# Scores from the seventh pair on as full 128-row matmuls, and V in four blocks

## The chip, the cores and the metric

The kernel runs on one core of a Trainium2 chip. The metric is the device time of one execution in microseconds (us). The core has a matrix engine (TensorE: PE for its matmuls, PEld for its weight loads), a vector engine (VectorE, DVE), a scalar engine (ScalarE, ACT), a general one (GpSimd, POOL) and a queue that issues all transfers of this kernel (SyncE, SP). The operands lie in SBUF (128 partitions); matmuls write to PSUM.

## The reference

Eight batches of twelve heads of attention with 448 positions and head size 64, with normalised queries and keys, and behind it a two-layer network without bias whose activation is h cos h:

```python
q_n, k_n = rmsnorm(q, g_q), rmsnorm(k, g_k)          # x / sqrt(mean(x*x) + 1e-6) * g
scores = q_n @ k_n.T / sqrt(64)
attn = exp(scores - max); attn = attn / (sum(attn) + 1e-9)
x = (attn @ v) with heads side by side               # 3584 x 768
h = x @ w_in                                         # 768 x 2048
out = (h * cos(h)) @ w_out                           # 2048 x 768
```

All is float32. The two weight matrices come as 64-bit numbers that the kernel turns into float32 itself.

## The kernel before

**Pairs.** Two heads make a pair `u`, 48 in all, six to a batch (NP = 6). Head 0 lies on partitions 0 to 63 of the transposed queries and keys, head 1 on 64 to 127. The 2 x 448 rows of queries are cut into seven tiles of 128: tiles 0 to 2 are head 0, tiles 4 to 6 head 1, and tile 3 is the last 64 rows of both, with the other head's part zero, so that it contracts over 128 partitions while the other six contract over 64.

**High and low parts.** The first six pairs are "plain": their matmuls take float32 operands. From the seventh pair on each operand is split into a high part (rounded to float32r) and a low part (the rest), and a product is three matmuls: high x high, low x high, high x low. `score` (L410) issues them for a pair of tiles (j, j + 4) in turn, so six matmuls with 64 contraction rows, or three for tile 3. I call the six a group; a pair has three groups.

**A pair's steps.** `st_load` to `st_pow` (L293 to L309) square and sum queries and keys and make 1/rms (`r`); `st_store` and `rk_load` send the keys' part through HBM and back as rows (`rkb`); `k_norm`, `k_high`, `k_low` and `q_scale`, `q_high`, `q_low` (L356 to L382) make the operands. After `score`, DVE scales each tile and takes its minimum (`rowmin`, L428), ACT takes the exponential and its row sums (`expo`, L435) into a tile `P`. `transp` (L459) turns the P tiles on PE in four column blocks kc of 128 (the last two overlap), seven transposes each; in block 1 one more transposes the row sums (L464), and DVE then adds 1e-9 and takes the reciprocal of the 7 x 128 result (`rs_copy`, L443). `pt_high` and `pt_low` split the turned block on ACT and DVE, and `av` (L481) multiplies it with V, which lies in five blocks per head (NVC): seven matmuls for a head, spread 2, 2, 1, 2 over the blocks.

**The network.** `ffn1` (L547) multiplies the previous batch's x with w_in in chunks fc of 128 columns, 18 matmuls a chunk, between the attention's steps; `weights` decodes w_in on DVE in four steps of a chunk (L210, L212, L214, L218), `weights2` makes seven sums of quarters of w_out. After the last pair a second plan runs the last batch's first layer and then the second layer (L613), as seven products for two batches.

**What sets the order.** `Plan` is a list scheduler that runs when the program is built. Each step is added with an engine, an assumed cost, a due time, what it reads and writes, and for transfers an assumed time to land; `order()` writes the steps down one after the other as they would start by these numbers, and this fixes the order of every engine and of SP's transfers. `RING` says how many buffers a name has. At run time each engine takes its instructions in that order and waits on semaphores. PSUM tile `PT` (two banks, L454) serves all transposes, and also the squares of the first two pairs' keys (`kn_square`).

Of the kernel before, what the change touches and what calls it, by code (L numbers as in the profile page):

```python
# [23 lines left out]
class Plan:  # L24
# [6 lines left out]
    SIGNAL = 0.16  # L31
# [33 lines left out]
    def order(self):  # L65
# [21 lines left out]
        while True:  # L87
# [35 lines left out]
def tile_attention_moe(  # L123
# [17 lines left out]
    NVC = 5  # L141
# [41 lines left out]
    def g_fold():  # L183
# [99 lines left out]
    pair = {}  # L283

# [29 lines left out]
    def kn_load(u):  # L314
        nc.sync.dma_start(tl(u, "kn", [128, 512], F32, "ql")[:KB], kn_in[u])
# [23 lines left out]
    def kn_copy(u):  # L339
        nc.scalar.activation(tl(u, "khi", [128, S], F32), kn_bank(u)[:, :S], AF.Copy, scale=gsc)  # L340
# [15 lines left out]
    def k_norm(u):  # L356
        kd = pair[u]["kd"]
        kn = tl(u, "khi", [128, S], F32) if u < NP else kd
        nc.gpsimd.tensor_tensor(kn, kd, pair[u].pop("rkb"), ALU.mult)
# [7 lines left out]

    def q_load(u):
        q = tl(u, "qhi" if u < NKT else "qd", [128, 512], F32)
        nc.sync.dma_start(q, qT[u])  # L370

    def q_scale(u):
        qd = pair[u]["qd"]
        q = tl(u, "qhi", [128, 512], F32) if u < NP else qd
        nc.gpsimd.tensor_scalar(q, qd, gsc, 0.0, op0=ALU.mult, op1=ALU.add)
# [34 lines left out]
    def score(u, j):  # L410
        d = pair[u]
        ops = (("qhi", "khi"), ("ql", "khi"), ("qhi", "kl"))[: 1 if u < NP else 3]
        if j == 0:
            tl(u, "sm", [128, 3, NQT], F32)
# [5 lines left out]
        for n, (a, c) in enumerate(ops):  # L420
            for t in tiles:
                p0, p1 = (0, 128) if t == 3 else (0, 64) if t < 3 else (64, 128)
                nc.tensor.matmul(  # L423
                    d["S", t][:, :S], d[a][p0:p1, j * 128 : j * 128 + 128], d[c][p0:p1, :],
                    start=(n == 0), stop=(n == len(ops) - 1),
                )
# [15 lines left out]

    def rs_copy(u):  # L443
        rt = tl(u, "rt", [NQT, 128], F32)
        nc.vector.tensor_scalar(rt, pt[:NQT, 896:1024], 1e-9, None, op0=ALU.add)
        nc.vector.reciprocal(rt, rt)
# [12 lines left out]
    def transp(u, kc, tiles, last):  # L459
        for t in tiles:  # L460
            src = pair[u][f"P{t}"][:, KS[kc] : KS[kc] + 128]
            nc.tensor.transpose(pt[:, t * 128 : t * 128 + 128], src, ident)  # L462
        if last:
            nc.tensor.transpose(pt[:NQT, 896:1024], pair[u]["sm"][:, 2, :], ident)  # L464

    def pt_high(u, kc, hh):
        d = pair[u]
        hi = d["hi", kc, hh] = apool.tile([128, S], F32R, tag="hi", name=f"hi{u}_{kc}_{hh}", bufs=RING["hi"])
        nc.scalar.copy(hi, pt[:, hh * S : hh * S + S])  # L469

    def pt_low(u, kc, hh):
# [6 lines left out]
        else:  # L478
            nc.vector.tensor_tensor(d["hi", 2, hh][:64], src[:64], hi.bitcast(F32)[:64], ALU.subtract)  # L479

    def av(u, kc, hh):  # L481
# [4 lines left out]
        ops = (((0, "hi", 0), (0, "lo", 0)), ((1, "hi", 1), (1, "lo", 1)), ((3, "lo", 2),), ((2, "hi", 3), (4, "hi", 2)))  # L486
        for n, (c, what, kb) in enumerate(ops[kc]):
            st = d["vs"][:, hh * NVC + c].rearrange("p a d -> p (a d)")
            nc.tensor.matmul(O, st, d.pop((what, kb, hh)), start=(kc + n == 0), stop=(kc + n == 4))  # L489

    def pt_copy(u, kc, hh):
        p = pair[u]["hi", kc, hh] = apool.tile([128, S], F32, tag="hi", name=f"hi{u}_{kc}_{hh}", bufs=RING["hi"])
        if hh:
            nc.vector.tensor_copy(p, pt[:, hh * S : hh * S + S])
        else:
            nc.scalar.copy(p, pt[:, hh * S : hh * S + S])

    def av_plain(u, kc, hh):
# [3 lines left out]
        p, st = d.pop(("hi", kc, hh)), d["vs"][:, hh * NVC + (0, 1, 3, 2)[kc]]  # L502
# [4 lines left out]
    xs = {}  # L507
# [153 lines left out]
    def weights(fc):  # L661
        d = ffn_due(0, 3 * fc) - 6.0
        w, f = ("w", fc), ("wf", fc)
        begin = 8.0 + 6.0 * fc
        add(SP, ISS, d - 30.0, w_load, fc, w=[w if f64 else f], land=8.0, start=begin)
        if f64:
            for step, eng, cost in ((0, DVE, 0.6), (1, DVE, 1.05), (2, DVE, 1.0), (3, ACT, 0.92), (4, DVE, 1.1)):
# [9 lines left out]
    def weights2(c):  # L677
# [4 lines left out]
        for k in range(4):  # L682
            st, f, e = ("wf", NFC + 4 * c + k), qk[k], d + 0.1 * span * k
            if f64:
                add(SP, ISS, e - 20.0, v_fetch, c, k, w=[st], land=LAND, start=e - 30.0)
                for step, eng, cost in ((0, DVE, 0.42), (1, DVE, 0.7), (2, DVE, 0.7), (3, ACT, 0.56), (4, DVE, 0.66)):
# [10 lines left out]
        for n, (name, src, _) in enumerate(SPLITS):  # L697
# [8 lines left out]
            add(ACT, 0.5, e, v_split, c, p, src, False, r=[f], w=[o])  # L706
# [3 lines left out]
    def prepare(u):  # L710
# [3 lines left out]
        if turned:  # L714
            kn, rn, kb = [("ql", u)], [("rn", u)], [("pt", 0, n) for n in ((0,) if u == 0 else (1, 2))]
# [6 lines left out]
            add(ACT, 0.53, D0 - 50, kn_copy, u, r=kb + [("gsc", 0)], w=khi)  # L722
# [3 lines left out]
        add(SP, ISS, D0 - 44 if turned else D0 - 30, q_load, u, w=qhi if turned else qd, land=3.5 if turned else LAND)  # L726
        add(ACT, 0.6 if turned else 0.95, D0 - 40, st_square, u, w=sd)
        add(DVE, 0.7 if turned else 1.08, D0 - 38, st_reduce, u, r=sd, w=r)
        add(POOL, 1.5 if turned else 2.6, D0 - 34, st_pow, u, w=r)
# [290 lines left out]
```

## Time and profile before

| | |
|---|---|
| median of 3 runs | 1469.57 us (1469.06 to 1471.99) |
| the profiled execution | 1471.15 us, of it the span from first to last instruction 1469.4 us |
| mean granted TensorE clock | 0.995 |
| PE, DVE, ACT, POOL busy | 96%, 75%, 62%, 46% of the span |
| transfers | 260.96 MB, mean 178 GB/s |

A row of the timeline gives start and duration of merged instructions (xN is their number), engine, line, operation, out<-in. Matmuls overlap their neighbours, so the time that one takes from the engine is the distance between starts, not its duration. A row of the groups ends with the busy time, the mean of one in ns, and the idle time before them. A row of the windows gives busy time and number of instructions of PE, PEld, DVE, ACT and POOL in that stretch, then the granted clock, the busy share of the transfer engines and GB/s.

### The profile page before, as it was taken

The page shows a single profiled execution, that of the slowest core. Times are in us where ns is not written, and L with a number is a line of the kernel's source. Part 1 is how long each engine was busy: PE and PEld are TensorE (multiplying, and loading weights), DVE is VectorE, ACT ScalarE, POOL GpSimd, SP SyncE. Part 2 cuts the span into 40 slices and gives each one's busy share as a digit, 9 for nine tenths or more (in the row PEclk, how much of TensorE's full clock was granted, in tenths as well). Part 3 has the DMA queues.
Part 4 walks back from the last instruction along what each step waited for, and adds up shares of the span by engine and source line. Part 5 has one row for each costly group of instructions (what it writes and reads, how often), then busy time and mean ns, then how long its engine had stood idle before and what let it go on. Part 6 is the DMA issues. An engine that isn't in the chain of part 4 may idle for free.

```text
span 1469.4 us, 22204 instructions
## 1 busy us (share of the span) xinstructions
PE 1407.9 (96%) x7370; PEld 1161.3 (79%) x7370; DVE 1103.2 (75%) x1861; ACT 915.1 (62%) x1820; POOL 669.0 (46%) x634
## 2 busy tenths in 40 slices
PE   5878999999999999999999999999999999999998
PEld 2334788878788878878887888878999999999998
DVE  6988898687868787777878666543958978979843
ACT  4666676767677776677776766545737547447421
POOL 4889874866776776686586765211000000000000
PEclk9999999999999999999999999999999999999999
DMA  6773344556445554646454533118948658568534
GB/s 228 223 221 117 121 129 131 184 165 210 154 153 176 179 183 148 196 145 195 157 192 157 177 111 98 59 45 310 300 159 278 229 162 303 197 193 308 162 106 142
DMA packets 135876, 260.96 MB, mean 178 GB/s; under 512 B 21792, under 2 KB 89968, under 8 KB 135760
## 3 DMA queue, kind: packets, MB, share of 16 engines
q1 hardware_dynamic: 135760, 259.53, 54.6%
q8 instruction: 58, 0.95, 0.3%
q14 instruction: 58, 0.48, 0.1%
HBM read 196.74 MB, written 62.73 MB: 177 GB/s over the span
## 4 chain that ended last, share of the span: by engine, by line
PE 81%; DVE 9%; POOL 3%; issue 3%; ACT 2%; DMA 2%; SPq 0%; POOLq 0%; ACTq 0%; DVEq 0%
PE y L625 9%; PE y L624 9%; PE y L623 9%; PE O L489 9%; PE ph L556 8%; PE PT L462 8%; PE ph L557 8%; PE ph L558 8%; PE S L423 7%; DVE S L430 2%; DVE lo L477 1%; PE y L557 1%; PE y L558 1%; PE y L556 1%; POOL r L309 1%
## 5 line engine op out<-in xcount | busy, mean ns | idle before, releaser
L438 ACT ACTIVATE P<-S,sm 128x448 f32<-128x448 f32 x336 | 213.7, 639 | 122.1 <-DVE S L430 118.4
L556 PE MATMUL ph<-xs,wi 128*128 128x448 f32 x672 | 263.6, 392 | 2.7 <-ACT he L568 2.7
L557 PE MATMUL ph<-xs,wi 128*128 128x448 f32 x672 | 247.1, 368 | 0.4 <-POOL xs L542 0.4
L558 PE MATMUL ph<-xs,wi 128*128 128x448 f32 x672 | 246.5, 367 | 0.0
L624 PE MATMUL y<-g,wo 128*128 128x448 f32 x672 | 245.6, 365 | 0.0
L625 PE MATMUL y<-g,wo 128*128 128x448 f32 x672 | 245.5, 365 | 0.0
L623 PE MATMUL y<-g,wo 128*128 128x448 f32 x672 | 245.5, 365 | 0.0
L430 DVE TENSOR_SCALAR_CACHE_REDUCE S<-S,r 128x448 f32<-128x448 f32 x336 | 220.4, 683 | 19.4 <-PE S L423 15.9
L469 ACT CAST hi<-PT 128x448 fp32r<-128x448 f32 x336 | 165.4, 535 | 91.1 <-PE PT L462 45.1
L603 ACT CAST g<-gq 128x896 fp32r<-128x896 f32 x112 | 105.7, 943 | 174.4 <-PE y L625 161.2
L477 DVE TENSOR_TENSOR lo<-PT,hi 128x448 fp32r<-128x448 f32 x252 | 143.1, 607 | 70.5 <-ACT hi L469 66.1
L601 DVE TENSOR_TENSOR g<-gq,g 128x896 fp32r<-128x896 f32 x112 | 122.1, 1090 | 83.8 <-ACT g L603 83.3
L462 PEld LDWEIGHTS PT<-ident,P 128*128 128x128 f32 x1344 | 157.7, 142 | 31.7 <-issue 20.0
L462 PE MATMUL PT<-ident,P 128*128 128x128 f32 x1344 | 182.5, 276 | 0.2 <-ACT P L438 0.2
L556 PEld LDWEIGHTS ph<-xs,wi 128*128 128x128 f32 x672 | 127.1, 189 | 27.7 <-issue 11.3
L558 PEld LDWEIGHTS ph<-xs,wi 128*128 128x128 f32 x672 | 126.7, 189 | 11.1
L623 PEld LDWEIGHTS y<-g,wo 128*128 128x128 f32 x672 | 126.3, 188 | 10.0
L625 PEld LDWEIGHTS y<-g,wo 128*128 128x128 f32 x672 | 126.3, 188 | 9.9
L624 PEld LDWEIGHTS y<-g,wo 128*128 128x128 f32 x672 | 126.3, 188 | 9.9
L557 PEld LDWEIGHTS ph<-xs,wi 128*128 128x128 f32 x672 | 127.3, 189 | 8.5 <-POOL xs L542 0.8
L309 POOL TENSOR_TENSOR r<-r,nhalf 128x14 f32<-128x14 f32 (+1 forms) x48 | 125.9, 2622 | 4.0
L489 PE MATMUL O<-hi,vs 128*128 128x448 f32 x336 | 113.2, 389 | 6.4 <-DVE hi L479 3.4
(94 smaller groups left out, 2569.4 us busy)
## 6 DMA issues: line engine op xcount, KB each, us to landing
wo<-wo_d SPq DMA_DIRECT2D x152, 384.0 KB
h_d<-he SPq DMA_DIRECT2D x128, 224.0 KB
gq<-h_d SPq DMA_DIRECT2D x64, 448.0 KB
wo_d<-ao SPq DMA_DIRECT2D x56, 384.0 KB
sd<-sd SPq DMA_DIRECT2D x46, 448.0 KB
vd<-v SPq DMA_DIRECT2D x84, 160.0 KB
raw<-w_in SPq DMA_DIRECT2D x16, 768.0 KB
rawo<-w_out SPq DMA_DIRECT2D x32, 384.0 KB
```

Source lines behind the costliest of these rows:

```text
L430: nc.vector.tensor_scalar(d["S", t][:, :S], d["S", t][:, :S], d["r"][:, t : t + 1], None, op0=ALU.mult, op1=ALU.min, accum_out=d["sm"][:, ...
L438: nc.scalar.activation(tl(u, f"P{t}", [128, S], F32, "P"), d.pop(("S", t))[:, :S], AF.Exp, bias=sm[:, 1, t : t + 1], scale=-1.0, accum_out ...
L462: nc.tensor.transpose(pt[:, t * 128 : t * 128 + 128], src, ident)
L469: nc.scalar.copy(hi, pt[:, hh * S : hh * S + S])
L477: nc.vector.tensor_tensor(lo, src, hi.bitcast(F32), ALU.subtract)
L489: nc.tensor.matmul(O, st, d.pop((what, kb, hh)), start=(kc + n == 0), stop=(kc + n == 4))
L556: nc.tensor.matmul(ph[:, :S], whi, x2[:, 0, :], start=(cc == 0), stop=False)
L557: nc.tensor.matmul(ph[:, :S], whi, x2[:, 1, :], start=False, stop=False)
L558: nc.tensor.matmul(ph[:, :S], wlo, x2[:, 0, :], start=False, stop=(cc == NCC - 1))
L623: nc.tensor.matmul(y, whi, hi[:, e], start=first and e == 0, stop=False, **more)
L624: nc.tensor.matmul(y, whi, lo[:, e], start=False, stop=False, **more)
L625: nc.tensor.matmul(y, wlo, hi[:, e], start=False, stop=last and e == NG - 1, **more)
```

## The change

From pair 6 on, the 64 contraction rows of a head are doubled to 128: `m_place` puts the keys' high part on partitions 0 to 63 and its low part on 64 to 127 of a tile `M`, `d_place` puts the queries' high part on both halves of a tile `D`, `e_place` puts the queries' low part on the upper half (0 to 63) of a tile `E` whose other half was set to zero at the start. One matmul D x M then gives high x high + high x low, and one E x M gives low x high: two matmuls with 128 rows for each of the six tiles, and still three for tile 3. The places are filled by transfers from SBUF to SBUF, ten of 64 partitions for a pair. `score` is now issued tile by tile; the plain pairs keep the old form (`score_plain`).

V lies in four blocks. The last transposed block (kc = 3) has 64 columns only, its high part on partitions 0 to 63 and its low part on 64 to 127 of one tile, against V rows that are stored twice; `av` is 2, 2, 2, 1 matmuls for a head.

The reciprocal of the row sums is taken before they are turned, on 128 x 7 numbers (`rsum`: an ACT step adds 1e-9, a DVE step takes the reciprocal); `rs_copy` only copies. The six plain pairs' queries have their own tile `q6` and are loaded at the start. The second pair's keys `kn` are loaded into another buffer than before. Loads of w_in start at other times, ring sizes and the plan's assumed costs change.

```diff
-    NVC = 5
+    NVC = 4
...
-        "sd": 1, "r": 5, "rkb": 1, "kd": 1, "kl": 2, "khi": 2, "qd": 1, "ql": 2, "qhi": 2, "vd": 1, "vs": 2, "S": 3, "sm": 3, "P": 12,
-        "hi": 4, "lo": 2, "O": 1, "xf": 6, "rs": 1, "rt": 1, "ph": 1, "he": 2, "wf": 2, "rn": 1,
-        "aq": 4, "at": 2, "ao": 2,
+        "sd": 1, "r": 5, "rkb": 1, "kd": 1, "kl": 1, "khi": 1, "qd": 1, "ql": 1, "qhi": 1, "M": 3, "D": 3, "E": 3, "vd": 1, "vs": 2, "S": 3, "sm": 3, "P": 11,
+        "hi": 4, "lo": 2, "O": 1, "xf": 6, "rs": 1, "rt": 1, "ph": 1, "xsb": 1, "he": 2, "wf": 2, "rn": 1,
+        "aq": 4, "at": 2, "ao": 1,
...
+    def m_place(u, h, low):
+        if not low:
+            pair[u]["M", h] = apool.tile([128, S], F32R, tag="M", name=f"M{u}_{h}", bufs=RING["M"])
+        src = pair[u]["kl" if low else "khi"].bitcast(F32)
+        nc.sync.dma_start(pair[u]["M", h].bitcast(F32)[64 * low : 64 * low + 64], src[64 * h : 64 * h + 64])
+
+    def d_place(u, h):
+        t = pair[u]["D", h] = apool.tile([128, 384], F32R, tag="D", name=f"D{u}_{h}", bufs=RING["D"])
+        src = pair[u]["qhi"].bitcast(F32)[64 * h : 64 * h + 64, :384]
+        for a in (0, 64):
+            nc.sync.dma_start(t.bitcast(F32)[a : a + 64], src)
...
+    ORDER = (3, 0, 4, 1, 5, 2, 6)
+
+    def score(u, n):
...
+            h, c = t // 4, t % 4 * 128
+            ops = tuple((d[name, h][:, c : c + 128], d["M", h]) for name in ("D", "E"))
+        for i, (a, c) in enumerate(ops):
+            nc.tensor.matmul(d["S", t][:, :S], a, c, start=(i == 0), stop=(i == len(ops) - 1))
...
-        rt = tl(u, "rt", [NQT, 128], F32)
-        nc.vector.tensor_scalar(rt, pt[:NQT, 896:1024], 1e-9, None, op0=ALU.add)
-        nc.vector.reciprocal(rt, rt)
+        nc.vector.tensor_copy(tl(u, "rt", [NQT, 128], F32), pt[:NQT, 896:1024])
...
     def transp(u, kc, tiles, last):
+        n = 128 if kc < 3 else 64
         for t in tiles:
-            src = pair[u][f"P{t}"][:, KS[kc] : KS[kc] + 128]
-            nc.tensor.transpose(pt[:, t * 128 : t * 128 + 128], src, ident)
+            src = pair[u][f"P{t}"][:, KS[kc] : KS[kc] + n]
+            nc.tensor.transpose(pt[:n, t * 128 : t * 128 + 128], src, ident)
...
-        begin = 8.0 + 6.0 * fc
+        begin = 4.0 + 3.0 * fc if fc < 3 else 24.0 + 7.0 * fc
...
-            kn, rn, kb = [("ql", u)], [("rn", u)], [("pt", 0, n) for n in ((0,) if u == 0 else (1, 2))]
+            kn, rn, kb = [("qd" if u == 0 else "ql", u)], [("rn", u)], [("pt", 0, n) for n in ((0,) if u == 0 else (1, 2))]
```

Three places of the order are spoken of below. The first is PE in the middle of the attention, where the score matmuls of a pair stand between chunks of the first layer (`ph`), products with V (`O`) and transposes (`PT`). Before, a group of two tiles:

```order
L558 MATMUL ph_11_5329<-xs,wi_1486 128x448
L423 MATMUL S_1_5386<-khi_5069,qhi_5106 128x448
L423 MATMUL S_5_5387<-khi_5069,qhi_5106 128x448
L423 MATMUL S_1_5386<-khi_5069,ql_5141 128x448
L423 MATMUL S_5_5387<-khi_5069,ql_5141 128x448
L423 MATMUL S_1_5386<-kl_5075,qhi_5106 128x448
L423 MATMUL S_5_5387<-kl_5075,qhi_5106 128x448
L489 MATMUL O_5400<-hi_0_0_5378,vs_5097 128x448
```

Now, tile 5 (head 1) and tile 2 (head 0) of a pair:

```order
L603 MATMUL ph_4_6321<-xs,wi_735 128x448
L465 MATMUL S_5_6426<-M_1_6205,D_1_6210 128x448
L465 MATMUL S_5_6426<-M_1_6205,E_100 128x448
L465 MATMUL S_2_6433<-M_0_6054,D_0_6065 128x448
L465 MATMUL S_2_6433<-M_0_6054,E_99 128x448
L534 MATMUL O_6306<-hi_2_0_6418,vs_5995 128x448
```

Six matmuls of 64 rows, two tiles by turns, became two matmuls of 128 rows for a tile, four for two tiles; the tiles of a pair need no longer stand together.

The second place is SP's first transfers (`kn`: keys of the first two pairs; `sd`: queries and keys for the sums of squares; `raw`: a chunk of w_in). Before:

```order
L315 DMA kn_101<-kn 112x512
L295 DMA sd_103<-sd 128x448
L370 DMA qhi_105<-qT 128x512
L181 DMA gs<-gg 128x2
L388 DMA vs_108<-v 128x640
L354 DMA kd_110<-kT 128x448
L370 DMA qd_112<-qT 128x512
L385 DMA vd_114<-v 128x320
L315 DMA kn_117<-kn 112x512
L370 DMA qhi_121<-qT 128x512
L295 DMA sd_128<-sd 128x448
```

Now:

```order
L322 DMA kn_108<-kn 112x512
L322 DMA kn_110<-kn 112x512
L302 DMA sd_112<-sd 128x448
L380 DMA q_98<-qT 128x512 x2
L181 DMA gs<-gg 128x2
L413 DMA vs_117<-v 128x512
L361 DMA kd_119<-kT 128x448
L380 DMA q_98<-qT 128x512 x4
L380 DMA qd_129<-qT 128x512
L410 DMA vd_134<-v 128x256
L199 DMA raw_138<-w_in 128x1536
L199 DMA raw_140<-w_in 128x1536
```

The second pair's keys moved from ninth to second place; the second pair's `sd`, eleventh before, now stands right behind these rows, with four more loads of queries and two chunks of w_in ahead of it.

The third place is ACT's first rows (`P`: exponentials of the first pair). Before:

```order
L318 ACTIVATE PT<-kn_101 112x512
L299 ACTIVATE sd_103<-sd_103 128x448
L318 ACTIVATE PT<-kn_117 112x512
L340 ACTIVATE khi_145<-PT,gs 128x448
L299 ACTIVATE sd_128<-sd_128 128x448
L438 ACTIVATE P_161,sm_149<-S_0_150,sm_149 128x448
```

Now:

```order
L325 ACTIVATE PT<-kn_108 112x512
L325 ACTIVATE PT<-kn_110 112x512
L306 ACTIVATE sd_112<-sd_112 128x448
L347 ACTIVATE km_158<-PT,gs 128x448
L306 ACTIVATE sd_142<-sd_142 128x448
L477 ACTIVATE P_182,sm_162<-S_0_163,sm_162 128x448
```

The square of the second pair's `sd` (`sd_128`, now `sd_142`) stands ahead of the first exponential in both.

More of the change, by code (lines that the diff above doesn't have):

```diff
@@ L24 @@
 class Plan:
-    SIGNAL = 0.16
+    SIGNAL = {"PE": 0.25, "ACT": 0.19, "DVE": 0.16, "POOL": 0.15, "SP": 0.16}
     LEAD = 0.3
@@ L283, in tile_attention_moe @@
     pair = {}
+    q6 = xpool.tile([128, NP, 512], F32, tag="xs", name="q6")
+    xs = {}
+    qlow = [apool.tile([128, 384], F32R, tag=f"E{i}", name=f"E{i}", bufs=1) for i in range(RING["E"])]
+    for t in qlow:
+        nc.vector.tensor_scalar(
+            t[64:128], ident[64:128, 0:1].broadcast_to([64, 384]), 0.0, 0.0, op0=ALU.mult, op1=ALU.add
+        )
     def tl(u, name, shape, dt, tag=None):
@@ L419, in score @@
             d["S", t] = pool.tile([128, 512], F32, tag=tag, name=f"S{u}_{t}")
[L420 to L426, printed above, removed]
+        for t in tiles:
+            p0, p1 = (0, 128) if t == 3 else (0, 64) if t < 3 else (64, 128)
+            q, k = q_plain(u)[p0:p1, j * 128 : j * 128 + 128], d["km"][p0:p1, :]
+            nc.tensor.matmul(d["S", t][:, :S], q, k, start=True, stop=True)
+    ORDER = (3, 0, 4, 1, 5, 2, 6)
+    def score(u, n):
+        d = pair[u]
+        if n == 0:
+            tl(u, "sm", [128, 4, NQT], F32)
+        t = ORDER[n]
+        d["S", t] = ps_s.tile([128, 512], F32, tag="S", name=f"S{u}_{t}")
+        if t == 3:
+            khi, kl = d["khi"], d["kl"]
+            qhi, ql = (d[name][:, 384:512] for name in ("qhi", "ql"))
+            ops = ((qhi, khi), (ql, khi), (qhi, kl))
+        else:
+            h, c = t // 4, t % 4 * 128
+            ops = tuple((d[name, h][:, c : c + 128], d["M", h]) for name in ("D", "E"))
+        for i, (a, c) in enumerate(ops):
+            nc.tensor.matmul(d["S", t][:, :S], a, c, start=(i == 0), stop=(i == len(ops) - 1))
     def rowmin(u, t):
@@ L685, in weights2 @@
                 add(SP, ISS, e - 20.0, v_fetch, c, k, w=[st], land=LAND, start=e - 30.0)
-                for step, eng, cost in ((0, DVE, 0.42), (1, DVE, 0.7), (2, DVE, 0.7), (3, ACT, 0.56), (4, DVE, 0.66)):
+                for step, eng, cost in ((0, DVE, 0.5), (1, DVE, 0.65), (2, DVE, 0.6), (3, ACT, 0.45), (4, DVE, 0.55)):
                     add(eng, cost, e + step, v_decode, c, k, step,
@@ L758, in attend, with soften @@
         lead = 0.0 if u < NP else None
+        inst = {}
+        def soften(t, n, key, due):
+            inst[t] = 7 * u + n
+            add(DVE, 0.61, due, rowmin, u, t, r=[("r", u)], w=[key, ("sm", u, 1, t)])
+            add(ACT, 0.62, due + 1, expo, u, t, r=[key, ("sm", u, 1, t)], w=[("P", inst[t]), ("sm", u, 2, t)])
         for j in range(4):
+            if not plain:
+                break
             tiles = (3,) if j == 3 else (j, j + 4)
@@ L762, in attend @@
             dj = D0 + step * j
[L763 to L770 removed]
+            add(PE, 1.1 if j < 3 else 0.92, dj, score_plain, u, j, lead=lead, r=[("qp", u), ("M", u), ("xsb", 0)], w=keys)
+            for n, t in enumerate(tiles):
+                soften(t, 2 * j + n, keys[n], dj + 1)
+        for n, t in enumerate(ORDER):
+            if plain:
+                break
+            key, dj = place(u, n), D0 + 0.5 * step * n
+            if t == 3:
+                r = [("qhi", u), ("ql", u), ("khi", u), ("kl", u)]
+            else:
+                i = 2 * u + t // 4
+                r = [("D", i), ("E", i), ("M", i - NP, 0), ("M", i - NP, 1)]
+            add(PE, 0.62 if t == 3 else 0.41, dj, score, u, n, lead=lead, r=r, w=[key])
+            soften(t, n, key, dj + 1)
         D1 = D0 + 4 * step
+        add(ACT, 0.2, D1, rsum, u, 0, r=[("sm", u, 2, t) for t in range(7)], w=[("sm", u, 3)])
+        add(DVE, 0.2, D1 + 1, rsum, u, 1, w=[("sm", u, 3)])
         for kc in range(4):
```

135 lines of the change are left out of this document (72 added, 63 removed).

## The prediction

> **What bounds the kernel now.** I read the page's first part, then the windows of three stages and of the start, PE's waits, and the timeline of PE where scores and transposes stand.
>
> ```profile
> span 1469.4 us, 22204 instructions
> PE 1407.9 (96%) x7370; PEld 1161.3 (79%) x7370; DVE 1103.2 (75%) x1861; ACT 915.1 (62%) x1820; POOL 669.0 (46%) x634
> ```
>
> ```profile
> 0.00:150.00 150.00, 111.90 (x453) 50.78 (x453) 123.70 (x225) 91.74 (x197) 112.30 (x97) 0.98 0.61 194
> 150.00:960.00 810.00, 793.18 (x4433) 648.67 (x4432) 613.71 (x1245) 564.10 (x1305) 547.66 (x530) 1.00 0.49 155
> 960.00:1470.00 510.00, 502.81 (x2487) 461.88 (x2487) 365.80 (x393) 259.25 (x320) 8.99 (x8) 1.00 0.63 208
> ```
>
> ```profile
> PE O L489 <- DVE lo L477: 13.2, 19, 2.0
> ...
> PE PT L337 <- ACT PT L318: 10.6, 1, 10.6
> ```
>
> Each window gives busy PE, PEld, DVE, ACT, POOL, then clock, transfer share and GB/s. From 150 to 960 us (pairs 6 to 47) PE is busy 98%, DVE 76%, ACT 70%, POOL 68%: PE's instruction stream is the bound, and time taken out of it comes off the end. The last 510 us aren't touched by the change. In the first 150 us PE is busy for 112 us only, and DVE, 124 us, is the fullest.
>
> **Scores.** A stretch of PE's timeline in the middle, a first-layer stream, a group of six score matmuls, then transposes:
>
> ```profile
> 505.24 0.37 PE L557 MATMUL ph<-xs,wi 128*128 128x448 f32 x1
> 505.45 0.37 PE L558 MATMUL ph<-xs,wi 128*128 128x448 f32 x1
> 505.75 0.47 PE L423 MATMUL S<-khi,qhi 64*128 64x448 f32 x2
> 506.05 0.37 PE L423 MATMUL S<-khi,ql 64*128 64x448 f32 x2
> 506.26 0.36 PE L423 MATMUL S<-kl,qhi 64*128 64x448 f32 x2
> 506.55 0.66 PE L462 MATMUL PT<-ident,P 128*128 128x128 f32 x4
> ```
>
> And a run of full matmuls and transposes, quoted here for their distances:
>
> ```profile
> 432.62 0.93 PE L462 MATMUL PT<-ident,P 128*128 128x128 f32 x7
> 433.38 0.27 PE L464 MATMUL PT<-ident,sm 128*7 128x128 f32 x1
> 433.41 0.45 PE L556 MATMUL ph<-xs,wi 128*128 128x448 f32 x1
> 433.70 0.37 PE L557 MATMUL ph<-xs,wi 128*128 128x448 f32 x1
> ...
> 435.77 0.37 PE L558 MATMUL ph<-xs,wi 128*128 128x448 f32 x1
> ...
> 436.79 0.93 PE L462 MATMUL PT<-ident,P 128*128 128x128 f32 x7
> 437.47 0.45 PE L556 MATMUL ph<-xs,wi 128*128 128x448 f32 x1
> 437.76 0.37 PE L557 MATMUL ph<-xs,wi 128*128 128x448 f32 x1
> ```
>
> A full 448-column matmul costs (435.77 - 433.70) / 10 = 0.207 us. The group: from the last `ph` at 505.45 to the transposes at 506.55 is 1.10 us, less 0.207 for that `ph`: 0.893 us. The two matmuls of a step run together (x2 in one distance), so three steps alone would be 0.62 us; the other 0.27 us are lost on entering (0.30 instead of 0.21), after the first step (0.30) and on leaving (0.29). Now the two tiles take four full matmuls: 4 x 0.207 = 0.828. Saved: 0.065 us in each of 42 x 3 = 126 groups, **-8.2 us**. Tile 3 is unchanged. A rule speaks against the change: the Trainium skill, "TensorE: Matmul & The Clock Gate", section "Why this matters for your kernels", says that matmuls with few contraction rows run concurrently when they lie in different row groups. By it alone a group is three streams, 0.62, and the scores' term is +0.207 x 126 = +26 us, not -8.2. The Trainium skill, "TensorEngine Tiling (Array Packing)", section "Key Properties", adds that changing the tiling mode drains the engine, with which the 0.09 us at either end agree.
>
> **Transposes of block 3.** They now turn 64 columns of P, not 128: 7 in each of 48 pairs. The trace has transposes of 7 columns, L464: from the first of seven to the second `ph` matmul behind them is 1.08 us with it (432.62 to 433.70) and 0.97 without (436.79 to 437.76), so the narrow one costs 0.11 us, what each of the others does ((433.38 - 432.62) / 7). A 64-column one lies between equal ends: I take **0**. The bound below is half price, 0.055 x 7 x 48 = 18.5 us. In the Trainium skill, same page, "LDWEIGHTS (loading the stationary operand)", load time goes with the columns; by it the transposes would be cheaper (a rival below), and L464's price speaks against it.
>
> **V in four blocks, the sums.** `av` stays at seven matmuls a head: 0 on PE. POOL's V copies shrink by a fifth, on an engine at 68%. On DVE the long reciprocal goes and a short one comes:
>
> ```profile
> L446 DVE RECIPROCAL rt<-rt 7x128 f32<-7x128 f32 x48 | 45.2, 941 | 1.6
> L184 DVE SCALAR_TENSOR_TENSOR gs<-gs 128x1 f32<-128x1 f32 x1 | 0.2, 159 | 0.7 <-DMA gs<-gg 0.7
> L438 ACT ACTIVATION_READ_ACCUMULATOR P<-S,sm 128x1 f32 x336 | 67.7, 202 | 0.0
> ```
>
> The new one is 7 numbers wide; nearest are a 1-wide DVE step, 0.16 us, and the old 0.94 for 128: I take 0.16. ACT gains about a 0.2 us step per pair, at 70%: hidden. DVE loses 0.78 us per pair, which stood just ahead of `pt_low`, the step for which PE waits 13.2 us in all. That wait can shrink by 0 to 13.2; I take **-2 us**, near zero because only one of a pair's four blocks had the reciprocal ahead of it.
>
> **Transfers.** Ten new issues a pair. Each stands at 0.38 us on SP (row below), 3.8 us of a pair's 810 / 42 = 19.3 us, and SP waits 207 us for `h_out` alone. They bring 4 x 115 + 6 x 98 = 1.05 MB a pair, 54 GB/s beside 155: by proportion the share goes from 0.49 to 0.66. A score tile can't start before its transfers land, and they wait in SP's order for POOL's low parts and for PE to leave the third buffer. Behind such a wait stand the loads of later pairs (`sd`, `kd`, `vd`), the rk and rs trips and `wo_d` and `h_d`. The nearest landing times: the first `kn`, issued at 0.72, is read at 3.41 (2.7 us, empty queue); the second, at 4.48, is read at 9.97 (5.5 us, behind 2.4 MB). The plan reckons 5 us, and its due times stand 10 to 14 us ahead of the pair's first tile. I take 0; the range keeps a loss (a rival).
>
> ```profile
> 0.72 0.40 SPq L315 DMA_DIRECT2D kn<-kn  x1
> ...
> 4.48 0.43 SPq L315 DMA_DIRECT2D kn<-kn  x1
> ...
> 506.14 0.38 SPq L385 DMA_DIRECT2D vd<-v  x1
> ```
>
> ```profile
> SPq L571 <- ACT he L568: 207.2, 94, 6.7
> ```
>
> ```profile
> 3.41 0.60 ACT L318 ACTIVATE PT<-kn 112x512 f32<-112x512 f32 x1 [1.42 <-DMA kn<-kn]
> ...
> 9.97 0.60 ACT L318 ACTIVATE PT<-kn 112x512 f32<-112x512 f32 x1 [5.46 <-DMA kn<-kn]
> ...
> 15.92 0.63 ACT L438 ACTIVATE P<-S,sm 128x448 f32<-128x448 f32 x1 [2.36 <-DVE S L430]
> ```
>
> ```profile
> L277 POOL TENSOR_TENSOR ao<-aq,ao 128x384 fp32r<-128x384 f32 x40 | 42.1, 1059 | 27.8 <-ACT ao L274 27.8
> ```
>
> One `ao` buffer for two costs 0: a turn is such a step, half of one on ACT and a store of 5.5 at most, 7 us, and 56 of them fill 390 of some 700 us; were they late, the second layer would wait for its weights. One P tile fewer is covered by the first layer's matmuls, 16 chunks for six pairs; without them PE would wait out one exponential (0.63 us in its row above) a pair.
>
> **The start.** PE's first transposes waited until 10.6 us for the square of the second `kn`, as both write `PT`:
>
> ```profile
> 6.80 0.69 DVE L332 TENSOR_TENSOR kn<-kn,rn 112x512 f32<-112x512 f32 x1 [0.64 <-POOL rn L327]
> ```
>
> ```profile
> 13.14 3.36 PE L423 MATMUL S<-khi,qhi 64*128 64x448 f32 x8 [1.50 <-ACT khi L340]
> ```
>
> With that `kn` second in the queue they can follow the normalised keys at 7.5, near 8, and the scores 2.5 us later, near 10.5 rather than 13.1. But the first exponential stands behind the square of the second pair's `sd`, and ahead of that lie now, by the order's rows, two `kn` and an `sd` (0.69 MB), seven queries (1.84), V and keys (0.62) and two chunks of w_in (1.57), with itself 4.95 MB. At the 318 GB/s of the first stretch (below) they take 15.6 us from 2 us on, and about 1 us to land: the first exponential comes near 19, not at 15.9, +3.1 us.
>
> ```profile
> 2.00:13.00 11.00, 1.01 (x4) 0.66 (x4) 2.76 (x5) 2.24 (x5) 4.47 (x6) 1.00 0.96 318
> ```
>
> ```profile
> L303 DVE TENSOR_REDUCE r<-sd 128x14 f32<-128x896 f32 x46 | 49.7, 1080 | 2.8 <-ACT sd L299 1.8
> L212 DVE SCALAR_TENSOR_TENSOR wf<-raw,wf 128x768 int32<-128x768 int32 x16 | 18.9, 1178 | 0.3
> L210 DVE TENSOR_SCALAR wf<-raw 128x768 int32<-128x768 int32 x16 | 15.3, 958 | 3.3 <-POOL wi L233 3.3
> ```
>
> From there DVE sets the pace:
>
> ```profile
> 49.62 0.67 DVE L430 TENSOR_SCALAR_CACHE_REDUCE S<-S,r 128x448 f32<-128x448 f32 x1
> ```
>
> That is pair 2's first minimum. Ahead of it DVE's order loses an L210 and an L212 (2.1 us), two reciprocals (1.6) and a reduction (1.1): -4.8. From there to the plain pairs' last copy it loses a net decode step of 1.2 and four reciprocals (3.1) and gains two reductions (2.2): -2.1. The three fills of `E` (0.5 us each by L210's rate) lie in DVE's idle time before the scores (2.8 of 11 us busy). Sum: 3.1 - 4.8 - 2.1 = **-4 us**. Bounds: -7 when the late `sd` is hidden, +6 when POOL's chain to pair 2's keys holds the gain back and the late start stays, with a first-layer start behind the plain scores.
>
> **Sum.** -8.2 - 2 - 4 = -14.2 us. The profiled execution took 1471.15, 1.6 above the median of three; it would become 1456.95, and the median 1455.4. About 0.2% (2.9 us) is what a measurement can tell from no change. Adding the terms' ends: -8.2 - 13 - 7 gives 1441, -8.2 + 6 gives 1467.
>
> **Rivals.** *Half-price transposes* (10%): the cost goes with the 64 columns; 18.5 us more come off, 1437. For it: the rule above; against it: L464.
>
> *The start loses* (12%): +6 instead of -4, 1465. For it: 4.95 MB ahead of `sd`; against it: DVE's shorter list.
>
> *Late places* (9%), the slower side: the score matmul of a head finds its `M`, `D` or `E` not landed, and PE, which takes its order as it stands, idles. 84 heads: from 0.17 us each the gain is gone, from 0.2 it is slower; at 0.5 us it is +42, 1497. For it: share 0.66 and one queue in order; against it: 10 us of lead for 2.7 to 5.5.
>
> *Concurrency lost* (3%): the 0.27 us of a group turn up with full matmuls too, as ends of waits. Then four streams replace three, +0.207 x 126 = 26 us, less 6: 1490. Against it: the loss stands in the group's own rows, without a releaser.
>
> *Saved but not on the path* (8%): PE waits out what it saves for the exponentials; only the start's part stays, 1466 or no change.
>
> **Numbers.** The forecast has 58% (its own range 1441 to 1467). Faster by over 0.2%: forecast, half price and nearly all of the start, 0.79; same, 0.08; slower, late places, lost concurrency and a remainder of the start, 0.13. The range 1437 to 1467 leaves out those and most of the no-gain case, nearly 2 in 10.
>
> **What would show it.** Right: tile scores of two matmuls at 0.207 each without the 0.09 on either side; 64-column transposes 0.11 apart; PE not waiting on transfers at the score line; first exponential near 19 us; the minimum of pair 2 near 48 (49.6 before); the middle stage 8 to 12 us shorter. Wrong: 0.055 between block 3's transposes, waits of PE for `M`, `D`, `E`, a stage before the first first-layer chunk that is longer, or a clock below 0.99.

## The result, and the profile after

| | before | after |
|---|---|---|
| median | 1471.60 us (5 runs, 1469.06 to 1474.71) | 1462.19 us (5 runs, 1459.68 to 1464.83) |
| the profiled execution | 1471.15 us, span 1469.4 us | 1460.98 us, span 1458.9 us |
| transfers | 260.96 MB | 301.87 MB |

The ratio is 0.9937, with a 95% interval from 0.9916 to 0.9957: 9.4 us less, inside the predicted range, where 14.2 were forecast. The page of the kernel after, its first part, and the windows of the same three stretches:

```profile
span 1458.9 us, 22540 instructions
...
PE 1389.1 (95%) x7118; PEld 1197.0 (82%) x7118; DVE 1085.6 (74%) x1864; ACT 915.4 (63%) x1868; POOL 647.8 (44%) x634
```

```profile
0.00:150.00 150.00, 118.02 (x469) 55.68 (x469) 118.62 (x230) 91.38 (x204) 112.62 (x98) 0.97 0.71 211
150.00:960.00 810.00, 778.01 (x4216) 687.17 (x4216) 607.45 (x1257) 570.76 (x1360) 526.19 (x529) 0.99 0.71 203
960.00:1470.00 510.00, 493.09 (x2436) 454.17 (x2434) 359.52 (x378) 253.28 (x306) 8.98 (x8) 1.00 0.63 207
```

PE has less to do, but it is no longer busy 98% of the middle stage: 778 of 810 us, 15 us less than before. The list of PE's waits shows what it waits for instead (total, times, longest, in us):

```profile
PE O L534 <- DVE lo L523: 9.5, 14, 1.7
...
PE S L447 <- ACT P L477: 6.0, 1, 6.0
...
PE S L465 <- issue: 3.7, 2, 3.4
...
PE S L465 <- DMA E<-ql: 2.7, 1, 2.7
PE PT L507 <- DVE lo L523: 2.3, 3, 1.0
...
PE S L465 <- DMA sd<-sd: 1.8, 1, 1.8
...
PE S L465 <- DMA rk_d<-r: 1.0, 1, 1.0
...
PE S L465 <- DMA rs_d<-rt: 0.8, 1, 0.8
...
PE S L465 <- DMA h_d<-he: 0.5, 1, 0.5
```

L465 is the score matmul on placed operands. Its waits for transfers (the name behind DMA is only the last landing that the profile can pair with it, and "issue" a wait for which it finds none) sum to 10.5 us; before there were none at that line. The wait of the products with V for DVE's `lo` fell from 13.2 to 9.5 us, but transposes now wait 2.3 us for it, and did not before. L447 is the score matmul of the plain pairs; its one wait of 6.0 us, for an exponential, is new too and belongs to the start.

Where the difference lies is best read from the start of the second layer, whose instructions the change leaves alone. The first row of its first matmul's line, before and after (duration, then first and last start):

```profile
L623 PE MATMUL y<-g,wo x178: 362/365/370, 1056.9 to 1164.6; 128*128 128x448 f32 x178
```

```profile
L668 PE MATMUL y<-g,wo x195: 362/365/369, 1046.6 to 1164.5; 128*128 128x448 f32 x195
```

It starts 10.3 us earlier, and the end comes 10.5 us earlier (span 1469.4 to 1458.9). From here on "first stage" means the time up to that row.

One thing must be known to read the totals that follow. The last batch's first layer and the second layer (2016 matmuls, between which PE never waits) run at one of two paces, settled for an execution. The window from 1170 to 1230 us of the changed kernel and of the same kernel run again:

```profile
1170.00:1230.00 60.00, 60.00 (x298) 55.61 (x297) 48.17 (x51) 35.07 (x40) 0.00 (x0) 1.00 0.69 222
```

```profile
1170.00:1230.00 60.00, 60.00 (x292) 54.50 (x291) 47.37 (x50) 34.20 (x39) 0.00 (x0) 1.00 0.67 214
```

298 or 292 matmuls in 60 us, 202.7 or 206.7 ns apart, at the same granted clock. Over the 412 us behind the first stage's end this is 8 us, and about 1 more in the last batch's first layer just ahead of it. It is a property of the execution, not of the kernel (the changed kernel shows both), so I compare first stages by traces, where the pace makes the difference of about 1 us, and give the medians beside them. The pace of an execution that was not traced is not known.

### The profile page after: what moved, and what is told of

Its sections match the earlier page's. It is cut to its first block, busy times and chain, and to the rows that moved or that the text cites. A ratio compares the mean times of both kernels' runs of the same rounds, so it can differ in the third digit from the quotient of the medians.

```text
span 1458.9 us, 22540 instructions
## 1 busy us (share of the span) xinstructions
PE 1389.1 (95%) x7118; PEld 1197.0 (82%) x7118; DVE 1085.6 (74%) x1864; ACT 915.4 (63%) x1868; POOL 647.8 (44%) x634
## 2 busy tenths in 40 slices
DMA packets 169477, 301.87 MB, mean 207 GB/s; under 512 B 28512, under 2 KB 123568, under 8 KB 169360
## 5 line engine op out<-in xcount | busy, mean ns | idle before, releaser
L515 ACT CAST hi<-PT 128x448 fp32r<-128x448 f32 (+1 forms) x336 | 165.4, 533 | 100.4 <-PE PT L507 55.4
L648 ACT CAST g<-gq 128x896 fp32r<-128x896 f32 x112 | 105.7, 943 | 174.9 <-PE y L670 161.6
L507 PE MATMUL PT<-ident,P 128*128 128x128 f32 (+1 forms) x1344 | 186.1, 275 | 6.6 <-ACT hi L515 3.5
L507 PEld LDWEIGHTS PT<-ident,P 128*128 128x128 f32 (+1 forms) x1344 | 155.6, 134 | 44.7 <-issue 18.2
L523 DVE TENSOR_TENSOR lo<-PT,hi 128x448 fp32r<-128x448 f32 x252 | 146.4, 615 | 41.0 <-ACT hi L515 38.9
L603 PEld LDWEIGHTS ph<-xs,wi 128*128 128x128 f32 x672 | 127.0, 189 | 11.2
L534 PE MATMUL O<-hi,vs 128*128 128x448 f32 x336 | 120.1, 372 | 3.6 <-DVE hi L525 1.4
```

Of the source, the lines that this page charges most:

```text
L507: nc.tensor.transpose(pt[:n, t * 128 : t * 128 + 128], src, ident)
L515: nc.scalar.copy(hi[:n], pt[:n, hh * S : hh * S + S])
L523: nc.vector.tensor_tensor(lo, src, hi.bitcast(F32), ALU.subtract)
L534: nc.tensor.matmul(O, st, d.pop((what, kc, hh)), start=(kc + n == 0), stop=(kc == 3))
L603: nc.tensor.matmul(ph[:, :S], wlo, x2[:, 0, :], start=False, stop=(cc == NCC - 1))
```

## The experiments

All are edits of the changed kernel. The table has the median of all runs, the ratio to the kernel before, which was run again beside each, with its interval, the first stage of the one traced execution, and the pace of its second layer.

| run | median, us | ratio (95%) | first stage, us | pace, ns |
|---|---|---|---|---|
| before | 1471.60 | | 1056.9 | 202.7 |
| after | 1462.19 | 0.9937 (0.9916 to 0.9957) | 1046.6 | 202.7 |
| `again` (unchanged) | 1463.86 | 0.9941 (0.9920 to 0.9963) | 1044.9 | 206.7 |
| `old_scores` | 1470.24 | 0.9987 (0.9971 to 1.0002) | 1048.0 | 202.7 |
| `old_scores_2` | 1464.56 | 0.9954 (0.9935 to 0.9973) | 1047.4 | 206.7 |
| `no_place` | 1460.90 | 0.9918 (0.9901 to 0.9934) | 1038.9 | 206.7 |
| `unread` | 1459.64 | 0.9904 (0.9886 to 0.9922) | 1035.4 | 206.7 |
| `old_recip` | 1498.33 | 1.0169 (1.0148 to 1.0189) | 1075.8 | 206.7 |
| `recip_true` | 1470.84 | 1.0002 (0.9982 to 1.0023) | 1056.6 | 202.7 |
| `old_costs` | 1472.89 | 1.0008 (0.9982 to 1.0033) | 1059.3 | 202.7 |
| `land8` | 1570.59 | 1.0682 (1.0651 to 1.0713) | 1157.9 | 202.7 |
| `m4_land8` | 1484.48 | 1.0085 (1.0062 to 1.0108) | 1064.9 | 206.7 |
| `old_begin` | 1451.11 | 0.9868 (0.9848 to 0.9889) | 1038.5 | 206.7 |
| `m4_begin_land7` | 1449.83 | 0.9863 (0.9842 to 0.9884) | 1033.6 | 202.7 |

My theory was the prediction's: the shorter score groups carry the gain and the placing transfers are hidden. The rival: PE's waits for the placed operands eat that gain, and what was measured comes from the rest of the change.

**The scores as before** (`old_scores`). The split pairs' `score` is the old one, six 64-row matmuls in turn:

```diff
-        for n, t in enumerate(ORDER):
...
+        for j in range(4):
...
+            add(PE, 0.88 if j < 3 else 0.62, dj, score, u, j, lead=lead, r=r, w=keys)
```

> The changed kernel with the scores of the split pairs as before: groups of six 64-row matmuls and the single tile 3, no M, D or E, two buffers each of khi, kl, qhi and ql; start, reciprocal, V in four blocks and costs as changed. Theory 1 (the shorter groups carry the gain, 126 x 0.065 = 8 us, and the placing transfers are hidden): about 1470 us, ratio to the kernel before 0.999. Theory 2 (PE's waits for M, D and E, some 9 to 11 us in seven places of the changed kernel's trace, eat that gain, and what was measured comes from the rest of the change): 1459 to 1463 us, as the changed kernel or a little below.

The median, 1470.2, was what the first theory named. The trace said otherwise: its execution took 1462.45, and its first stage 1048.0, 1.4 us more than after. Ten other executions lay from 1469 to 1474, and one took 2251 us, for a reason that nothing here shows (the expectation below counts it among those near 1470). The run was made once more for a second trace:

> The run with the old scores once more, for a second trace. Its profiled execution took 1462 us, with matmuls of the second layer 202.7 ns apart; eleven others took 1469 to 1474. If those eleven had the second layer's matmuls at 206.7 ns (theory 2: net of PE's waits for the placed operands, the new scores bring under 2 us in the first stage), a trace of an execution near 1470 us shows 206.7 and a first stage that ends within 3 us of 1048. If they were longer in the first stage (theory 1, the new scores bring their 8 us), such a trace shows 202.7 and a first stage that ends near 1056.

This time the traced execution took 1469.96 us, and its window reads:

```profile
1170.00:1230.00 60.00, 60.00 (x292) 54.50 (x291) 47.75 (x51) 32.57 (x38) 0.00 (x0) 1.00 0.67 213
```

292 matmuls, 206.7 ns: the 8 us lie in the second layer, and the first stage again ends at 1047.4. The other ten executions fall into two bunches, 1459.2 to 1464.6 and 1468.8 to 1470.0. So the rival holds: in the whole first stage the new form of the scores with its places is worth 1.4 us against the old one at the faster pace (1048.0 against 1046.6) and 2.5 at the slower (1047.4 against 1044.9 of `again`), about as much as two traces of the changed kernel differ by, 1.7. The pages show where it goes: at the faster pace PE is busy for 1405.2 us with the old scores and for 1389.1 after, 16.1 less, but idle for 14.3 us more.

**The places left out, and the places unread** (`no_place`, `unread`). In both, D x M and E x M read one tile that is filled once, so that six of seven score tiles of the split pairs are not computed from queries and keys. The first drops the ten transfers of a pair; the second issues them, and nothing reads what they bring:

```diff
-            ops = tuple((d[name, h][:, c : c + 128], d["M", h]) for name in ("D", "E"))
+            ops = tuple((still[:, c : c + 128], still) for name in ("D", "E"))
...
-                r = [("D", i), ("E", i), ("M", i - NP, 0), ("M", i - NP, 1)]
+                r = []
```

> The changed kernel with the ten placing transfers of a pair left out: the two matmuls of a tile score read one tile that is filled once at the start, so six of seven score tiles of the split pairs are not computed from queries and keys. Instructions on the five engines are else those of the changed kernel, 420 transfers fewer. Theory 1: 1459 to 1462 us, within 2 us of the changed kernel. Theory 2: 1450 to 1455 us, 7 to 11 us below it, and no wait of PE at the score line on a transfer.

> As the run without the placing transfers, but they are issued and land, and nothing reads what they place (six of seven score tiles are again not computed from queries and keys). Theory 1: 1459 to 1462 us. Theory 2: if the cost is PE's wait for a landing, as low as without the transfers, 1450 to 1455 us; if it is what 420 more transfers do to the loads on the same queue, near the changed kernel's 1462.

By the medians the first theory would have it (1460.9 and 1459.6); but both traces are of the 206.7 pace, and their first stages end at 1038.9 and 1035.4, which is 7.7 and 11.2 us sooner than after. Their lists of PE's waits have none at the score line on a transfer. Three things follow. The new form by itself, with no operands to wait for, is 8.5 us shorter than the old by `no_place` and 12.0 by `unread` (1038.9 and 1035.4 against the 1047.4 of the same pace); 8.2 were predicted. The need to wait for the operands gives back 7.7 to 11.2 against the first trace of the changed kernel, and 6.0 to 9.5 against `again`, which ran at their pace: over 84 heads 0.07 to 0.13 us a head. And it is the waiting, in the run and in the order that is planned around it, not what the 44 MB (168 x 96, 168 x 112 and 84 x 96 KB) take from other work: the run that moves them unread is not longer than the one without them. In it no place waits for PE to leave a buffer either, so the two waits are not told apart. PE has the same work in both runs, and their first stages differ by 3.5 us: so much can come from the order alone, and each row is one trace.

**The old reciprocal** (`old_recip`, `recip_true`). The turned sums' reciprocal is taken by DVE on 7 partitions again; the second run also tells the plan what the two instructions take:

```diff
-        nc.vector.tensor_copy(tl(u, "rt", [NQT, 128], F32), pt[:NQT, 896:1024])
+        rt = tl(u, "rt", [NQT, 128], F32)
+        nc.vector.tensor_scalar(rt, pt[:NQT, 896:1024], 1e-9, None, op0=ALU.add)
+        nc.vector.reciprocal(rt, rt)
...
-                add(DVE, 0.28, dk + 1, rs_copy, u, r=[("pt", 0, 2)], w=[("rt", u)])
+                add(DVE, 0.5, dk + 1, rs_copy, u, r=[("pt", 0, 2)], w=[("rt", u)])
```

(`recip_true`: 1.22 in place of 0.5.)

> The changed kernel with the reciprocal as before: turned sums, 1e-9 added and the reciprocal taken by DVE on 7 partitions x 128, no step on ACT. Theory 1: the term of the prediction, 2 us more (1464 us), at most 4. Theory 2: a larger part of the gain, 3 to 6 us more (1465 to 1468 us), since PE's wait for DVE's lo fell by 3.7 us in the trace.

> The run with the old reciprocal (1498 us), with its two DVE instructions reckoned in the plan at what the trace shows, 1.22 us, instead of 0.5. Theory A (the order is planned on costs that are now exact, so that one step reckoned 0.7 us too short makes every lo behind it late): 1464 to 1472 us. Theory B (1.2 us of DVE between a pair's copies and lo are themselves on PE's path): 1490 to 1498 us.

Neither theory had 1498. The wait of PE's products with V for `lo`, in the first run and in the second:

```profile
PE O L536 <- DVE lo L525: 24.0, 35, 2.7
```

```profile
PE O L536 <- DVE lo L525: 12.8, 23, 2.0
```

With the old instructions and the old reckoning of 0.5 us, first stage 29.2 us longer (about 1 of it the slower pace); with the same instructions reckoned at 1.22 us, 10.0 longer (1056.6 against 1046.6). So about two thirds of the damage is the wrong number in the plan (theory A), and the step itself is worth 10 us, not 2. The kernel before had the same 0.5 and waited only 13.2 us for `lo`. A reading that fits, and was not tried by itself: its other costs were too long (0.7 us for a minimum that takes 0.61 in the new plan, 0.94 for an exponential, now 0.62), so its order left room into which the missing 0.7 us fell.

**The old costs** (`old_costs`). The assumed costs of the steps that both kernels have, the due times of the operands' steps and the signal time as before, with the changed instructions:

```diff
-    SIGNAL = {"PE": 0.25, "ACT": 0.19, "DVE": 0.16, "POOL": 0.15, "SP": 0.16}
+    SIGNAL = dict.fromkeys(("PE", "ACT", "DVE", "POOL", "SP"), 0.16)
...
-            add(DVE, 0.61, due, rowmin, u, t, r=[("r", u)], w=[key, ("sm", u, 1, t)])
+            add(DVE, 0.7, due, rowmin, u, t, r=[("r", u)], w=[key, ("sm", u, 1, t)])
```

> The changed kernel with the plan's old costs and its one signal time of 0.16 us; instructions on the engines the same, in the order that these costs give. Theory 1 (the gain is the scores'): 1460 to 1465 us, as changed. Theory 2 (the costs carry a part of it): 1466 to 1475 us.

First stage 12.7 us longer than after, the whole gain and more. No instruction differs, only the order. The run doesn't tell costs from due times: by the old ones the operands' steps come up to 6 us later (`q_low` 8 us ahead of its pair, not 14), in part behind the due times of the transfers that place what they make. PE's wait for `lo` is twice that of after:

```profile
PE O L534 <- DVE lo L523: 18.0, 23, 1.9
```

**The changed kernel again** (`again`), for the two paces:

> The changed kernel, unchanged, beside the three others on one chip. In the traces so far the second layer's 2400 matmuls stand 202.7 ns apart in some executions (the kernel before, the changed kernel, the run with the old scores) and 206.7 ns in others (the two runs without placed operands, the old reciprocal), from its first matmul to its last, which is 8 us. If that is settled per execution and not by the kernel, this run's second layer takes 412 or 420 us, whichever it falls into, the stage ahead of it agrees with the first trace within 3 us, and the median is 1459 to 1466 us. If it goes with the kernel's program: 412 us again.

It fell into the 206.7 pace, with 420.3 us behind a first stage of 1044.9: settled per execution. (The second layer has 2016 matmuls; the 2400 of the expectation is too many.)

**Places reckoned later, and a fourth M** (`land8`, `m4_land8`).

```diff
-            add(SP, ISS, D0 - 14 + 2 * h, m_place, u, h, 0, r=khi, w=[("M", m, 0)], land=LAND)
+            add(SP, ISS, D0 - 14 + 2 * h, m_place, u, h, 0, r=khi, w=[("M", m, 0)], land=8.0)
```

(and so for the other three; `m4_land8` has "M": 4 and "hi": 3 besides.)

> The changed kernel with the placing transfers reckoned in the plan at 8 us from issue to landing instead of 5, so that PE's order puts other work ahead of a score whose operands are late. Theory 1 (places are hidden): 1460 to 1464 us, as changed. Theory 2 (PE waits 9 to 11 us for them, as the middle stage of the two runs without them, 8 to 11 us shorter up to the second layer, says): 1452 to 1458 us, and the waits of the score line on transfers gone.

> The run that reckons the placing transfers at 8 us (1571 us), with four buffers of M instead of three (and three of hi instead of four, to make room). Theory C (with three M for two heads a pair, a head's key copy must wait until the head three before it has been scored, so that a longer reckoned landing stretches the whole period of a pair in the order): most of the 107 us comes back, 1480 to 1505 us. Theory D (the order is bad because scores are put off, however many buffers there are): 1550 to 1575 us.

The waits at L465 on transfers did go, but 111 us came in their place. PE's longest waits in `land8`, and its window from 160 to 940 us:

```profile
PE O L534 <- DVE lo L523: 25.3, 42, 1.4
PE O L534 <- DVE hi L525: 15.0, 21, 1.7
PE ph L601 <- ACT he L613: 13.7, 20, 1.8
PE O L534 <- ACT hi L515: 12.1, 18, 1.4
```

```profile
160.00:940.00 780.00, 712.33 (x3617) 602.92 (x3616) 514.33 (x1081) 491.12 (x1154) 466.51 (x466) 0.96 0.66 189
```

PE is busy 712 of 780 us, where after has 753, with many short waits for DVE and ACT, as if dependent steps now stood too close together (a reading of the waits, not shown step by step). A fourth buffer of `M` brings back 93 of the 111 us (1157.9 to 1064.9): theory C, inside its band. With three buffers for two heads a pair, the plan can't fill `M` for a head before the head three places ahead is scored, and a longer landing then stretches its whole cycle. I had seen the transfers' lateness and not this limit.

**Weights begun as before** (`old_begin`).

```diff
-        begin = 4.0 + 3.0 * fc if fc < 3 else 24.0 + 7.0 * fc
+        begin = 8.0 + 6.0 * fc
```

> The changed kernel with the loads of the first-layer weights begun as before, at 8 + 6 n in the plan, not at 4, 7, 10 and then later. Theory (two weight loads of 0.79 MB ahead of the second pair's sd make the first exponential wait until 20.8 us): the exponential comes near 17 us, and if the first pairs are on the path of everything behind them the end comes 3 to 5 us sooner (1457 to 1460 us). Rival (the first stage's DVE and the weights' own decoding set its end): no change, or 2 to 4 us more, since the decoding then falls among the first split pairs.

The first exponential in ACT's timeline, in the kernel after and here:

```profile
20.28 0.58 ACT L306 ACTIVATE sd<-sd 128x448 f32<-128x448 f32 x1 [8.95 <-DMA sd<-sd]
20.76 0.62 ACT L477 ACTIVATE P<-S,sm 128x448 f32<-128x448 f32 x1
```

```profile
15.75 0.58 ACT L306 ACTIVATE sd<-sd 128x448 f32<-128x448 f32 x1 [4.21 <-DMA sd<-sd]
16.23 0.62 ACT L477 ACTIVATE P<-S,sm 128x448 f32<-128x448 f32 x1
```

4.5 us sooner, and the first stage 8.1 us shorter (6.4 against `again`, which had the same pace), more than either side expected. But the 4.5 us aren't the 8: pair 2's first minimum comes at 52.3 us (50.4 after) and pair 6's at 105.1 (104.7), so the start alone is no further on. The lead shows from pair 9 on (172.4 against 179.3), and PE's waits at the score line, here, are:

```profile
PE S L465 <- DMA E<-ql: 1.8, 2, 1.3
...
PE S L465 <- DMA wo_d<-ao: 1.1, 1, 1.1
PE S L465 <- DMA rs_d<-rt: 0.4, 1, 0.4
```

3.3 us in place of 10.5: 7 us of waits for placed operands are gone, and more of them come in time in this order of loads. The lists don't add up to the 8 us by these alone: the wait at L447 falls from 6.0 to 1.6 us, and the one at L534 for DVE's `hi` grows from 1.4 to 6.1. Of the 10.5 us, 5.2 are two waits at 136 and 156 us, while the changed kernel is still loading w_in (its last chunk is issued at 142.4 us, here at 105.7); which chunk held which place was not taken apart further.

**A version to beat both** (`m4_begin_land7`): the three edits above together, 7 us in place of 8.

> The changed kernel with four buffers of M and three of hi, the placing transfers reckoned at 7 us, and the weight loads begun as before: a version meant to beat both. If PE's waits for placed operands (5 us from 160 to 940 us, and 6 more before that) and the late start are what is left: 1450 to 1457 us. If the order pays for the longer reckoning elsewhere, as waits for DVE's lo: 1460 to 1475 us.

1449.83 us, ratio 0.9863 (0.9842 to 0.9884), the shortest of all; first stage 1033.6. Its list of PE's waits has no row for L465 (the longest landing of the keys' low part is 6.9 us in its trace, inside the 7 reckoned), and the wait for `lo` stays near that of after:

```profile
PE O L534 <- DVE lo L523: 11.7, 19, 2.0
```

Against `old_begin` alone (0.9868) the medians don't tell them apart; the traces' first stages do by 4.9 us, one trace each and about 1 of it the pace.

## Why the prediction came out as it did

The range and the sign held, but the sum was right for partly wrong reasons: the scores with their places, which were to bring 8.2 of 14.2 us, bring about 2, and the steps put at nothing or 2 us carry the rest. That the errors of the terms nearly cancel is luck. Two of the prediction's own signs of being wrong came: waits of PE for `M`, and a stage up to the first first-layer chunk that is longer, 110.8 us (109.9 before).

**Scores, -8.2: the mechanism is right, the size about so, and little is left of it.** The timeline in the middle of the changed kernel:

```profile
510.44 0.37 PE L603 MATMUL ph<-xs,wi 128*128 128x448 f32 x1
510.65 0.37 PE L465 MATMUL S<-M,D 128*128 128x448 f32 x1
510.85 0.37 PE L465 MATMUL S<-M,E 128*128 128x448 f32 x1
511.06 0.36 PE L534 MATMUL O<-hi,vs 128*128 128x448 f32 x1
```

0.20 to 0.21 us each, no entry and no exit: as foreseen. Without the need for places the first stage is 8.5 us (`no_place`) or 12.0 us (`unread`) shorter than with the old scores. That the first is so near 8.2 is partly luck: by the pages PE is busy for 14.8 us less in `no_place` than in `old_scores_2`, not 8.2, and idle for 6.0 more; where the rest of the 14.8 comes from was not taken apart. The rule that would have made it +26 (concurrent row groups, three streams of 0.62) is answered by the same runs.

**Ten placing transfers, 0: the step that failed.** The prediction put them at nothing, since the plan reckons 5 us and the due times lie 10 to 14 ahead, and kept "late places" as a rival with 9%. They cost 6 to 11 us, by 0.07 to 0.13 us a head, not the 0.5 of that rival. The mechanism is the rival's: a late place, and PE, which takes its order as it stands, idles. The longest of these waits, in the timeline of the changed kernel, SP's rows and then PE's:

```profile
782.86 0.47 SPq L302 DMA_DIRECT2D sd<-sd  x1
783.42 0.39 SPq L280 DMA_DIRECT2D wo_d<-ao  x1
783.86 0.42 SPq L244 DMA_DIRECT2D rawo<-w_out  x1
784.34 0.66 SPq L397 DMA_DIRECT2D M<-kl  x1
...
789.65 0.46 SPq L407 DMA_DIRECT2D E<-ql  x1
...
791.71 0.45 PE L465 MATMUL S<-M,D 128*128 128x448 f32 x1 [2.67 <-DMA E<-ql]
```

The name in brackets misleads. By the semaphore updates in the trace that `E` is complete only at 793.56, while the last part of `M<-kl`, the keys' low part, comes in at 791.58, just before PE starts: 7.2 us after its issue, behind three transfers of 448, 384 and 384 KB, in a stretch in which the transfer engines are busy 0.90 of the time (0.71 in the whole middle stage). All seven waits for transfers at this line end like this, at the landing of an `M<-kl` that was issued at most 2.7 us behind an `sd` of 448 KB. These seven took 4.0 to 7.2 us to land (the median of all 84 is 4.0), and they were issued only 0.6 to 6.1 us before PE stood ready for them. So both numbers of the step failed: the landing is not 2.7 to 5.5 us where it counts, and the lead is not the 10 to 14 us of the due times; six of the seven leads are 4.7 to 6.1 us, near the 5 us at which the plan reckons a place. With 7 us reckoned (`m4_begin_land7`) no such wait is left. The Trainium skill, "DMA: Bandwidth & Descriptors", section "Anatomy of one DMA", gives a transfer a fixed cost of about 2 us whatever its size, most of it the receipt of the last write (fitted there for GpSimd's queue). The quickest places here, 96 KB, land 2.0 us after their issue, which agrees. The late ones take 2 to 5 us more; I put that down to the large transfers just ahead of them, which was not tried by itself. SP can add to the lateness: its transfers use eight semaphores in turn, and an issue waits until the eighth transfer before it has landed (the `E` above, issued at 789.65, waited for the `wo_d` of 783.42, which landed at 789.59).

**Transposes of 64 columns, 0: right.** Seven of them, up to the next matmul, take 0.68 us, as seven of 128 columns did before (436.79 to 437.47); the rival at half price falls.

```profile
492.43 0.93 PE L507 MATMUL PT<-ident,P 128*64 128x128 f32 x7
493.11 0.45 PE L465 MATMUL S<-M,D 128*128 128x448 f32 x1
```

**The reciprocal, -2: the mechanism right, the size wrong.** The step that replaces 0.94 us costs 0.20 us on DVE (0.16 was taken), and PE's wait for `lo` shrank by 3.7 us in the products with V, by 1.4 with the transposes counted. Undone, it costs 10 us where the plan knows its length, five times the term and inside its bound of 13. The argument that fails is that only one of a pair's four blocks had the reciprocal ahead of it; that a late `lo` shifts everything behind it on DVE, not one block, is my reading, not shown step by step.

```profile
L487 DVE RECIPROCAL sm<-sm 128x7 f32<-128x7 f32 x48 | 9.5, 198 | 1.9 <-ACT sm L485 0.8
```

**The plan's costs: no term at all.** The change lists them, and the prediction gave them no line. By `old_costs` they are worth 12.7 us together with the due times, more than any other part. They add no instruction and take none away; they decide how far apart a step and the step that needs it stand.

**The start, -4: the wrong way.** PE's first transposes, and pair 2's first minimum:

```profile
9.63 0.98 PE L344 MATMUL PT<-ident,kn 112*128 112x112 f32 x4 [9.63 <-DMA q<-qT]
```

```profile
50.39 0.69 DVE L469 TENSOR_SCALAR_CACHE_REDUCE S<-S,r 128x448 f32<-128x448 f32 x1 [2.52 <-PE S L447]
```

The first turn came at 9.63 us ("near 8" was forecast, 10.63 before), the first exponential at 20.8 ("near 19"; 4.95 MB ahead of `sd` was the right count, the landing some 2 us slower), pair 2's minimum at 50.4 (48 forecast, 49.6 before). What was gained at the first turn is lost again in PE's wait of 6.0 us at L447 for the late exponential. So the first 50 us lose 0.8 us instead of gaining 4, and by `old_begin` the weights' new beginning costs 6 to 8 us up to the second layer, near the +6 of the start's bad end, though by another path: most of it stands in the list as waits for placed operands.

**Undone one at a time, the parts don't add up:** scores with places 2, reciprocal 10, costs 12.7, less 8 for the weights' beginning, make about 17, and 10.3 were measured. They meet in one order. V in four blocks was not undone; its copies on POOL fell from 0.92 to 0.78 us and from 0.52 to 0.48, on an engine at 44%.

## What to carry to other kernels

In a kernel whose order is written at build time from assumed costs, a step's assumed length is as real a part of it as its instructions: one step reckoned 0.7 us too short cost 18 to 19 us, and a landing reckoned 3 us longer cost 111 where three buffers closed the cycle. So cost a change of such a table as a part of its own. And when an operand comes by a transfer, reckon its landing by the large transfers that stand just ahead of it in the queue and look for the buffer that limits how early it can be asked for; the mean landing, and the due time, say little. And compare two kernels at a point of the trace ahead of any stretch that has a pace of its own.

## What the runs showed of the hardware that was not expected

Matmuls back to back (128 rows, 448 columns, PE without a wait) stand 202.7 or 206.7 ns apart for the whole of a 400 us stretch, at a granted clock of 1.00 in either case. The same kernel shows both (`old_scores` 202.7, `old_scores_2` 206.7); in the first stage, where PE is interrupted often, the mean is near 204 in every trace. What sets it was not found. The totals of `old_scores_2` lie in two bunches some 8 us apart, of which one execution of the upper was traced (206.7), and a median can land in either.

Transfers of one kind and size on one queue took 2.2 to 7.2 us from issue to landing (`M<-kl`, 112 KB, 84 of them in the changed kernel), the longest right behind larger ones.

The granted clock from 160 to 940 us was 0.96 in `land8`, where PE was busy least (712 us), against 0.99 in the kernel after (753). Idle time alone doesn't set it: `old_recip`, busy for 737 us there, had 1.00.
